# Moving the token scatters and two routing steps behind the first expert slot's set-up, and picking its token lists with bf16 matmuls

## The chip, the cores and the metric

One Trainium2 chip, one core. The metric is the device time of one launch in microseconds. The median of three runs of the kernel before is 1223.27 us.

## The reference, cut to what matters

Eight batches of eight heads, 576 tokens of 64 each, give 4608 tokens of 512 numbers. The kernel computes three things one after the other:

```python
q_s = softmax(q, axis=-1); k_s = softmax(k, axis=2)
x = einsum('bhsd,bhde->bhse', q_s, einsum('bhsd,bhse->bhde', k_s, v))   # x: 4608 x 512
logits = x @ w_gate + modality_bias[modality_id]                        # 8 experts
e_idx = argmax(logits, axis=1); gate_w = softmax(logits)[arange(N), e_idx]
out[mask] = gate_w[mask, None] * (relu(x[mask] @ w1[e]) @ w2[e])        # mask = (e_idx == e), 512 -> 1024 -> 512
return ((out @ m2_w1) * (out @ m2_w2)) @ m2_w3 @ m2_w_out
```

Each token goes to one expert only. So the kernel has to collect the tokens of an expert before it can multiply them.

## The kernel before

**The order of the work.** A small planner, `Plan`, takes every step with its engine, an estimated cost, the keys it reads and writes and a priority. It places the steps on the engines by these estimates, and each engine then runs its steps strictly in that order. A step that the planner puts too early therefore blocks what stands behind it on its engine.

**Attention and routing.** The tokens come in four chunks of two batches (`c` from 0 to 3). Each chunk has nine `attend` steps (L394 on): TensorE transposes the softmaxed queries (L399) and multiplies them (L412), ScalarE and VectorE evict the result (L422 to L425), SyncE stores x to DRAM (L429). After a chunk, `route(c)` (L441 on) adds up the logits and finds the argmax on VectorE (L450 to L458), gets every token's rank within its expert by ten bf16 matmuls (L463, L465) into PSUM bank 4, and computes positions (L468 to L472) and gate weights (L473 to L475). `scatters(c)` (L477) then writes the pairs (token number, gate weight) to `order_dram`, sorted by expert, with nine indirect DMAs of GpSimd (L436): 36 in all.

**Expert slots.** An expert slot (`slot`, L664 on) takes up to 512 tokens of one expert. SyncE loads the expert's weights (L697). GpSimd gathers the tokens' rows of x by four indirect DMAs (L706). ScalarE multiplies them by the gate weight (L710). TensorE transposes them (L726). To use the fast float32 form of matmul, weights and tokens are split in a high and a low part: by ScalarE (L677, L730) and by VectorE or, for two of eight W1 and W2 pieces, by GpSimd (L679, L731). Then come the first product with 96 matmuls (L743), the relu with its split (L747, L748), the second product with 96 matmuls (L763), and the stores (L773).

**The opening slots.** Slots 0 to 2 take only tokens of the first four batches, so they start before the attention of the later batches is finished. They don't read `order_dram`. `early_lists` (L564 on) builds their token lists on the chip. `A` (L595, six VectorE operations) has a one where a token's position modulo 128 fits a row, `same` (L599) where its block fits, `Bv` (L602, two operations) is `same` times the token number and times the gate weight. `pick` (L605 to L609) multiplies them, 18 float32 matmuls of 128x24 into bank 4:

```python
        for i, x in enumerate((ids, gate)):
            lv(vt_(n * nb), lambda i=i, x=x: V.tensor_tensor(Bv[:, :, :, i], same, x.unsqueeze(2).to_broadcast([128, n, nb]), op=ALU.mult), r=["same", "ids"] + [K("gate", c) for c in range(BEARLY // 2)], w=[K("Bv", i)])
```

The token numbers are then copied out (L612), which releases slot 0's gathers, and the gate weights too (L613). Slots from 3 on read their list from `order_dram` (L690), so the first of these loads needs all 36 scatters.

**The main program** (L836 to L905) adds, in this order: the four chunks with `route(c - 1)` inside chunk c, the scatters of chunks 0 to 2, slot 0, `route(3)`, the scatters of chunk 3, the table for the later slots (`main_table`, L615), slots 1 and 2, and the first steps of slots 3 and 4. Twelve conversions of dense weights (`doubles`, L779 on; GpSimd's part is L793) fill gaps. A branch follows (L886, L887), and after it the other slots and the dense products.

Of the kernel before, what the change touches and what calls it, by code (L numbers as in the profile page):

```python
# [20 lines left out]
E = 8  # L21
NT = 9
# [120 lines left out]
def body(tc, q, k, v, mod, wgate, mbias, w1, w2, m1, m2, w3, wo, out):  # L143
# [296 lines left out]

    def route(c):  # L441

# [6 lines left out]
        vv = lambda f, r=(), w=(), n=72: P.add("V", vt_(n), f, r=kk(r), w=kk(w))  # L449
        vv(lambda: V.tensor_tensor(l2_, l2_, rq_.unsqueeze(3).to_broadcast([128, H, NT, E]), op=ALU.mult), r=rqk, w=l2k, n=576)  # L450
        vv(lambda: V.tensor_reduce(l, l2_.rearrange("p h t e -> p t e h"), axis=AX.X, op=ALU.add), r=l2k, w=["l"], n=576)
# [38 lines left out]
    def vv(f, r=(), w=()):  # L490
        P.add("V", 0.15, f, r=list(r), w=["tbl"] + list(w), pri=tpri[0])
# [71 lines left out]
    def early_lists():  # L563
# [13 lines left out]

        A, Bv, same = part(n, 128), part(n, nb, 2), part(n, nb)
        io, ii, mf, mi, bf, bi, ids = part(128), part(128).bitcast(I32), part(n), part(n).bitcast(I32), part(n), part(n).bitcast(I32), part(n)
        first, fi, blocks = part(NE), part(NE).bitcast(I32), part(NE, 4)  # L580
# [18 lines left out]
        lv(vt_(n * nb), lambda: V.tensor_tensor(same, bf.unsqueeze(2).to_broadcast([128, n, nb]), blocks.rearrange("p a b -> p (a b)").unsqueeze(1).to_broadcast([128, n, nb]), op=ALU.is_equal), r=["blocks", "bf"], w=["same"])  # L599
        gate = tok[:, :, 1].bitcast(F32)  # L600
        for i, x in enumerate((ids, gate)):
            lv(vt_(n * nb), lambda i=i, x=x: V.tensor_tensor(Bv[:, :, :, i], same, x.unsqueeze(2).to_broadcast([128, n, nb]), op=ALU.mult), r=["same", "ids"] + [K("gate", c) for c in range(BEARLY // 2)], w=[K("Bv", i)])  # L602
        got = bank[4][:, 0 : 2 * nb]

# [3 lines left out]

        P.add("P", 2.5, pick, r=[K("A", c) for c in range(n // 3)] + [K("Bv", i) for i in range(2)] + kk, w=[K("bk", 4)])  # L609
        pv = got.rearrange("p (s t o) -> p s t o", s=NE, o=2)  # L610
        oks = [K("ord", i) for i in range(3)]
        lv(0.1, lambda: V.tensor_copy(ordt[:, 0:NE, :, 0], pv[:, :, :, 0]), r=[K("bk", 4)], w=oks)  # L612
        lv(0.1, lambda: V.tensor_copy(ordt[:, 0:NE, :, 1].bitcast(F32), pv[:, :, :, 1]), r=[K("bk", 4)], w=oks + kk)  # L613

# [49 lines left out]
    def slot(P, n, after=(), parts="lsab", T=None, again=False):  # L664
# [11 lines left out]
        def split(nm, i, raw, hi, lo, extra):  # L676
            P.add("S", sb_(512), lambda: SC.copy(hi(), raw()), r=[K(nm + "r", i), extra], w=[K(nm + "h", i)])  # L677
            e, g, c = (G, "G", gt_(512)) if i in (3, 7) else (V, "V", vt_(512))
            P.add(g, c, lambda: e.tensor_tensor(lo(), raw(), hi().bitcast(F32), op=ALU.subtract), r=[K(nm + "r", i), K(nm + "h", i), extra], w=[K(nm + "l", i)])  # L679

# [31 lines left out]
        if "s" in parts:  # L712
# [3 lines left out]
            for h in hs:  # L716
                for kp in range(2):
                    pb, ch = (5, 7)[kp], slice(TS * h, TS * h + TS)
                    p = bank[pb].rearrange("p (k t) -> p k t", k=2)
                    sl = slice(2 * kp, 2 * kp + 2)  # L720

                    def tr(kp=kp, p=p, h=h):
                        for kk in range(2):
                            for t in range(2):
                                c = 128 * (2 * kp + kk)
                                PE.transpose(p[:, kk, 128 * t : 128 * t + 128], xg[h][:, t, c : c + 128], ident)  # L726

                    P.add("P", 0.46, tr, r=[K("xg", h, 0), K("xg", h, 1)], w=[K("bk", pb)], pri=-230)
                    hi, lo = (lambda sl=sl, ch=ch: XT(0)[:, sl, ch]), (lambda sl=sl, ch=ch: XT(1)[:, sl, ch])
                    P.add("S", ps_(512), lambda hi=hi, p=p: SC.copy(hi(), p), r=[K("bk", pb), "Mb"], w=[K("xh", h, kp)], pri=-230)  # L730
                    P.add("V", vt_(512), lambda hi=hi, lo=lo, p=p: V.tensor_tensor(lo(), p, hi().bitcast(F32), op=ALU.subtract), r=[K("bk", pb), K("xh", h, kp)], w=[K("xl", h, kp, "t")], pri=-230)  # L731

# [106 lines left out]
    for c in range(4):  # L839
        load("k", c + 2)  # L840
        keys(c + 1)
        if c:
            route(c - 1)
# [16 lines left out]
    scats = lambda n: [K("scat", c) for c in range(NT * n // 2)]  # L860
    for c in range(3):
        scatters(c, ["Mb"])
    slot(P, 0)
    route(B // 2 - 1)
    scatters(3, ["Mb"])
    tpri[0] = 250
# [410 lines left out]
```

## Time and profile before

| what | value |
|---|---|
| median of three runs | 1223.27 us (1221.51 to 1226.41) |
| the profiled execution | 1225.3 us, span 1223.2 us |
| granted TensorE clock, mean of the span | 0.965 of full speed |
| TensorE busy | 1144.1 us, 94% |
| VectorE, ScalarE, GpSimd busy | 855.1 us (70%), 526.3 us (43%), 539.0 us (44%) |

The span is what the profile covers, and the time of the execution is 2.1 us longer. "Releaser" is what ended an engine's wait, as far as the profile can tell; "issue" means that the engine waited for nothing that the profile shows. A clock of 1.00 is TensorE's 2.4 GHz, 0.50 is 1.2 GHz.

### The profile page before, as it was taken

The numbers are of one execution on the slowest core, as the hardware profiler recorded it, in microseconds if no ns is written. First come the engines' busy times: TensorE is split into PE (matmuls) and PEld (weight loads), VectorE is DVE, ScalarE is ACT, GpSimd is POOL, SyncE is SP. The second block draws the span as 40 slices with busy tenths as digits, with TensorE's granted clock in tenths as the row PEclk, the third lists the DMA queues.
The fourth block names the chain that finished last, engine by engine and source line by source line (L and its number), as shares of the span: only waits on it lengthen the run. The fifth ranks groups of instructions, "written<-read, shape, count | busy, mean of one in ns | idle before, by whom it ended". The sixth has DMA issues, their size and how long they took to land.

```text
span 1223.2 us, 22923 instructions
## 1 busy us (share of the span) xinstructions
PE 1144.1 (94%) x8623; PEld 1040.8 (85%) x8623; DVE 855.1 (70%) x1435; ACT 526.3 (43%) x1003; POOL 539.0 (44%) x538
## 2 busy tenths in 40 slices
PE   3777879999989999999999999999999999999996
PEld 3666758778878888888987999999999999999996
DVE  6979768798468778778675757575666689765550
ACT  3545355434335444443463332424232445555550
POOL 0444248764133333323151355455555476443332
PEclk9878779999999999999999999999999999999998
DMA  9982464955246556445664334343443347987741
GB/s 355 390 309 81 136 204 145 187 178 211 99 137 206 168 181 197 157 164 181 208 204 141 100 110 136 101 141 110 128 124 116 97 147 246 341 266 236 234 140 51
DMA packets 156139, 216.00 MB, mean 177 GB/s; under 512 B 19790, under 2 KB 90994, under 8 KB 156018
## 3 DMA queue, kind: packets, MB, share of 16 engines
q1 hardware_dynamic: 148946, 195.00, 49.4%
q0 software_dynamic: 7072, 19.44, 5.2%
q8 instruction: 69, 1.13, 0.4%
q14 instruction: 52, 0.43, 0.1%
HBM read 156.35 MB, written 74.82 MB: 189 GB/s over the span
## 4 chain that ended last, share of the span: by engine, by line
PE 67%; DVE 2%; issue 1%; DMA 1%; ACT 0%; POOL 0%; SPq 0%; DVEq 0%; POOLq 0%; ACTq 0%
PE pb L1089 29%; PE pb L1222 14%; PE pb L763 12%; PE pb L743 10%; PE pb L982 2%; DVE ar L1016 2%; PE pb L726 1%; DMA ca<-p_dram 0%; DMA p_dram<-ca 0%; PE pb L969 0%; DVE ar L958 0%; POOL out_dram L1196 0%; DVE tt L958 0%; DVE al L958 0%; ACT al L957 0%
## 5 line engine op out<-in xcount | busy, mean ns | idle before, releaser
L1089 PE MATMUL pb<-al,ar 128*128 128x384 f32 x1728 | 309.3, 337 | 1.1 <-ACT sx L1095 0.8
L1089 PEld LDWEIGHTS pb<-al,ar 128*128 128x128 f32 x1728 | 301.7, 188 | 1.8 <-ACT sx L1095 1.1
L763 PE MATMUL pb<-ar 128*128 128x512 f32 (+1 forms) x960 | 215.2, 383 | 0.0
L743 PE MATMUL pb<-ar 128*128 128x512 f32 (+1 forms) x960 | 213.8, 383 | 1.0 <-DVE ar L748 0.5
L743 PEld LDWEIGHTS pb<-ar 128*128 128x128 f32 x960 | 174.4, 190 | 36.5 <-issue 1.3
L763 PEld LDWEIGHTS pb<-ar 128*128 128x128 f32 x960 | 174.3, 190 | 33.3
L1222 PE MATMUL pb<-ar 128*128 128x256 f32 x1512 | 182.6, 283 | 1.5 <-issue 0.7
L1222 PEld LDWEIGHTS pb<-ar 128*128 128x128 f32 x1512 | 181.8, 192 | 2.3 <-DVE ca L1236 0.8
L958 DVE TENSOR_TENSOR ar<-ca,ar 128x512 fp32r<-128x512 f32 x140 | 108.1, 779 | 53.6 <-ACT ar L957 42.9
L957 ACT CAST ar<-ca 128x512 fp32r<-128x512 f32 x140 | 86.2, 622 | 44.4 <-DMA ca<-p_dram 14.2
L747 ACT ACTIVATE ar<-pb 128x512 fp32r<-128x512 f32 (+1 forms) x80 | 46.1, 578 | 117.0 <-PE pb L743 110.6
L793 POOL TENSOR_TENSOR ca<-ca 128x512 f32<-128x512 f32 x40 | 56.2, 1405 | 85.3 <-DVE ca L792 71.3
L1095 ACT COPY sx<-pb 128x384 f32<-128x384 f32 x96 | 46.0, 481 | 91.8 <-PE pb L1089 55.5
L748 DVE SCALAR_TENSOR_TENSOR ar<-pb,ar 128x512 fp32r<-128x512 f32 (+1 forms) x80 | 52.6, 658 | 40.4 <-ACT ar L747 40.3
L330 POOL TENSOR_TENSOR kt<-kt,kr 128x384 f32<-128x384 f32 x36 | 44.3, 1267 | 76.0 <-ACT kr L324 76.0
L1123 POOL TENSOR_TENSOR ca<-ca 128x384 f32<-128x384 f32 x48 | 53.6, 1116 | 47.3 <-DVE ca L1123 47.3
L679 DVE TENSOR_TENSOR ar<-w2r,ar 128x512 fp32r<-128x512 f32 x60 | 46.1, 794 | 34.2 <-ACT ar L677 26.5
L1098 POOL TENSOR_TENSOR ca<-ca,sx 128x384 f32<-128x384 f32 x24 | 27.2, 1135 | 95.7 <-ACT sx L1095 95.7
L766 ACT COPY yo<-pb 128x512 f32<-128x512 f32 (+1 forms) x40 | 22.6, 565 | 107.7 <-PE pb L763 91.3
L679 POOL TENSOR_TENSOR ar<-w1r,ar 128x512 fp32r<-128x512 f32 x20 | 26.9, 1347 | 76.9 <-ACT ar L677 74.3
L1095 ACT COPY ca<-pb 128x384 f32<-128x384 f32 x48 | 23.0, 481 | 87.2 <-PE pb L1089 87.2
L706 POOL DMA_INDIRECT ca<-x_dram,ord x38 | 40.0, 1052 | 43.5 <-DVE ord L612 23.2
(276 smaller groups left out, 1816.4 us busy)
## 6 DMA issues: line engine op xcount, KB each, us to landing
p_dram<-ca SPq DMA_DIRECT2D x168, 192.0 KB
ca<-p_dram SPq DMA_DIRECT2D x126, 256.0 KB
w1r<-in_moe_w_dram SPq DMA_DIRECT2D x10, 2048.0 KB
w2r<-in_moe_w_dram SPq DMA_DIRECT2D x10, 2048.0 KB
ca<-in_moe_w_dram SPq DMA_DIRECT2D x32, 512.0 KB
kt<-in_k_dram SPq DMA_DIRECT2D x8, 1152.0 KB
qt<-in_q_dram SPq DMA_DIRECT2D x8, 1152.0 KB
vt<-in_v_dram SPq DMA_DIRECT2D x8, 1152.0 KB
```

The source lines that it names most:

```text
L679: P.add(g, c, lambda: e.tensor_tensor(lo(), raw(), hi().bitcast(F32), op=ALU.subtract), r=[K(nm + "r", i), K(nm + "h", i), extra], w=[K(nm ...
L743: PE.matmul(p(), lhsT=W1(i)[:, TURN[kk], ms], rhs=XT(z)[:, kk, cols], start=(kk == 0 and c == 0), stop=(kk == 3 and c == 2))
L747: P.add("S", ps_(N), lambda hh=hh, p=p: SC.activation(hh(), p(), AF.Relu), r=[K("bk", pb), "Mb"], w=[K("hh", h, m) for h in hs])
L748: P.add("V", vt_(N), lambda hh=hh, hl=hl, p=p: V.scalar_tensor_tensor(out=hl(), in0=p(), scalar=0.0, in1=hh().bitcast(F32), op0=ALU.max, o ...
L763: PE.matmul(p(), lhsT=W2(i)[:, f, ns], rhs=HT(y)[:, f, cols], start=(f == 0 and c == 0), stop=(f == 7 and c == 2))
L793: P.add("G", gt_(512), lambda: G.tensor_tensor(Tf, Tf, Qf, op=ALU.add), r=[K("Q", b)], w=[K("T", b)])
L957: P.add("S", (ps_ if psum else sb_)(n), lambda: SC.copy(hi(), src), r=sk, w=[hk])
L958: P.add("V", vt_(n), lambda: V.tensor_tensor(lo(), src, hi().bitcast(F32), op=ALU.subtract), r=list(sk) + [hk], w=[lk])
L1089: PE.matmul(bk(j), lhsT=Mt[:, f, a, i, m, t], rhs=X(y, x)[:, t], start=(fresh and t == 0 and n == 0), stop=(t == 1 and n == 2), skip_group ...
L1095: P.add("S", ps_(HB), lambda j=j, to=to: SC.copy(S(to), bk(j)), r=[bkk(j)], w=[sk(to)])
L1123: P.add(eng, c(HB), lambda: e.tensor_tensor(t[:, sl], x, y, op=op), r=kk, w=[k_])
L1222: PE.matmul(bk(j), lhsT=At[z][:, m, i, f], rhs=Bt[:, x, y, f], start=(fresh and f == 0 and n == 0), stop=(f == 3 and n == 2), skip_group_c ...
```

## The change

The numbers of lines move by 9 (L706 becomes L715, L743 becomes L752, and so on).

- The scatters of all four chunks are added after slot 0, and each reads the new key "cast". Slot 0's last GpSimd split of W1 writes that key.
- `route(2)` and `route(3)` are both added after slot 0. Their first step reads the new key "opened", which slot 0's split of the transposed tokens writes.
- `early_lists` breaks token numbers into two bf16 parts and gate weights into three. `A` and `Bv` are bf16. One VectorE operation of 1080 elements per partition makes `Bv`, and `pick` becomes 18 bf16 matmuls of 128x60. The parts are added up again by two reductions, one for the token numbers with a copy behind it, one for the gate weights.

```diff
-    def route(c):
+    def route(c, after=()):
...
-        vv(lambda: V.tensor_tensor(l2_, l2_, rq_.unsqueeze(3).to_broadcast([128, H, NT, E]), op=ALU.mult), r=rqk, w=l2k, n=576)
+        vv(lambda: V.tensor_tensor(l2_, l2_, rq_.unsqueeze(3).to_broadcast([128, H, NT, E]), op=ALU.mult), r=rqk + list(after), w=l2k, n=576)
...
-        A, Bv, same = part(n, 128), part(n, nb, 2), part(n, nb)
+        A, Bv, same = part(n, 64).bitcast(BF16), part(n, nb * 5 // 2).bitcast(BF16).rearrange("p a (b o) -> p a b o", o=5), part(n, nb)
...
+        lv(0.1, lambda: V.tensor_copy(xx[:, 0], ids), r=["ids"], w=["xx0"])
+        lv(0.1, lambda: V.tensor_tensor(xx[:, 1], ids, xx[:, 0], op=ALU.subtract), r=["ids", "xx0"], w=["xx1"])
+        lv(0.1, lambda: V.tensor_copy(xx[:, 2], gate), r=gk + kk, w=["xx2"])
+        lv(0.1, lambda: V.tensor_tensor(rest, gate, xx[:, 2], op=ALU.subtract), r=gk + ["xx2"], w=["rest"])
+        lv(0.1, lambda: V.tensor_copy(xx[:, 3], rest), r=["rest"], w=["xx3"])
+        lv(0.1, lambda: V.tensor_tensor(xx[:, 4], rest, xx[:, 3], op=ALU.subtract), r=["rest", "xx3"], w=["xx4"])
...
-        for i, x in enumerate((ids, gate)):
-            lv(vt_(n * nb), lambda i=i, x=x: V.tensor_tensor(Bv[:, :, :, i], same, ...
-        got = bank[4][:, 0 : 2 * nb]
+        lv(vt_(5 * n * nb), lambda: V.tensor_tensor(Bv, same.unsqueeze(3).to_broadcast([128, n, nb, 5]), xx.rearrange("p o a -> p a o").unsqueeze(2).to_broadcast([128, n, nb, 5]), op=ALU.mult), ...
+        got = bank[4][:, 0 : 5 * nb]
...
-        P.add("P", 2.5, pick, ...
+        P.add("P", 1.6, pick, ...
...
-        lv(0.1, lambda: V.tensor_copy(ordt[:, 0:NE, :, 0], pv[:, :, :, 0]), r=[K("bk", 4)], w=oks)
-        lv(0.1, lambda: V.tensor_copy(ordt[:, 0:NE, :, 1].bitcast(F32), pv[:, :, :, 1]), r=[K("bk", 4)], w=oks + kk)
+        lv(0.1, lambda: V.tensor_reduce(found, pv[:, :, :, 0:2], axis=AX.X, op=ALU.add), r=[K("bk", 4)], w=["found"] + kk)
+        lv(0.1, lambda: V.tensor_copy(ordt[:, 0:NE, :, 0], found), r=["found"], w=oks)
+        lv(0.1, lambda: V.tensor_reduce(ordt[:, 0:NE, :, 1].bitcast(F32), pv[:, :, :, 2:5], axis=AX.X, op=ALU.add), r=[K("bk", 4)], w=oks + kk)
...
-            P.add(g, c, lambda: e.tensor_tensor(...), r=[...], w=[K(nm + "l", i)])
+            P.add(g, c, lambda: e.tensor_tensor(...), r=[...], w=[K(nm + "l", i)] + (["cast"] if (n, nm, i) == (0, "w1", 7) else []))
...
-                    P.add("V", vt_(512), ..., w=[K("xl", h, kp, "t")], pri=-230)
+                    P.add("V", vt_(512), ..., w=[K("xl", h, kp, "t")] + ([K("opened")] if n == 0 else []), pri=-230)
...
-        if c:
+        if c in (1, 2):
             route(c - 1)
...
-    for c in range(3):
-        scatters(c, ["Mb"])
     slot(P, 0)
-    route(B // 2 - 1)
-    scatters(3, ["Mb"])
+    for c in (2, 3):
+        route(c, [K("opened")])
+    for c in range(4):
+        scatters(c, ["cast"])
```

The planner makes new orders out of this. On VectorE, in the run-up to `pick`, before:

```order
L451 TENSOR_REDUCE ca<-ca 128x72
L598 TENSOR_TENSOR qt_129<-qt_129 128x12
L452 TENSOR_TENSOR ca<-ca 128x72
L599 TENSOR_TENSOR qt_129<-qt_129 128x216
L453 TENSOR_REDUCE m_96<-ca 128x9
L602 TENSOR_TENSOR qt_129<-qt_129 128x216
L602 TENSOR_TENSOR qt_129<-qt_129,tid 128x216
```

and now, up to the copy that releases the gathers (L621):

```order
L605 TENSOR_SCALAR qt_129<-tab 128x3
L424 RECIPROCAL ca<-ca 128x8
L606 CAST qt_129<-qt_129 128x3
L425 TENSOR_TENSOR ca<-pp_83,ca 128x512
L607 TENSOR_TENSOR qt_129<-qt_129 128x12
L424 RECIPROCAL ca<-ca 128x8
L608 TENSOR_TENSOR qt_129<-qt_129 128x216
L425 TENSOR_TENSOR ca<-pp_82,ca 128x512
L609 TENSOR_TENSOR qt_129<-qt_129 128x1080
L385 TENSOR_TENSOR qs_134<-qt_130,qx_132 128x8x3x64
L620 TENSOR_REDUCE qt_129<-pb_75 128x12
L621 CAST ord<-qt_129 128x12
```

The steps of `route(2)` (L450 to L453 among them) are gone from here, and two evictions of attention (L424, L425) stand ahead of `pick`'s last operand instead; before, they stood behind it. A product of queries (L385) that stood behind the copy of the token numbers now stands ahead of it, and in the full order an L424 and a third L425 too, which this excerpt leaves out.

On TensorE around `pick`, as one piece of the difference (pp is an attention result, pb_75 is bank 4):

```order
 L399 MATMUL pb_78<-ident,qs_133 128x128 x4
-L607 MATMUL pb_75<-qt_129 128x24 x18
 L412 MATMUL pp_83<-bd_153,qT_137 64x73 x4
 L412 MATMUL pp_83<-bd_154,qT_137 64x73 x4
```

```order
 L412 MATMUL pp_82<-bd_153,qT_135 64x73 x4
 L412 MATMUL pp_82<-bd_154,qT_135 64x73 x4
+L614 LDWEIGHTS qt_129
+L614 MATMUL pb_75<-qt_129 128x60
```

The pair of L614 stands there 18 times. Two attends (64 matmuls, L412) that stood behind `pick` now stand ahead of it. The ten rank matmuls of `route(2)`, which came one transpose later, moved into slot 1's first product, beside those of `route(3)`.

On GpSimd, from slot 0's gathers on, before:

```order
L706 DMA ca<-x_dram,ord 128x512 x4
L436 DMA order_dram<-tid,pi 37376x2
L435 MEMSET nop 128x1
L436 DMA order_dram<-tid,pi 37376x2
L435 MEMSET nop 128x1
L436 DMA order_dram<-tid,pi 37376x2
L435 MEMSET nop 128x1
L436 DMA order_dram<-tid,pi 37376x2
L679 TENSOR_TENSOR ar<-w1r,ar 128x512 x2
```

and now:

```order
L715 DMA ca<-x_dram,ord 128x512 x4
L688 TENSOR_TENSOR ar<-w1r,ar 128x512 x2
L436 DMA order_dram<-tid,pi 37376x2
L435 MEMSET nop 128x1
L436 DMA order_dram<-tid,pi 37376x2
L715 DMA ca<-x_dram,ord 128x512 x2
```

The four scatters between slot 0's gathers and its splits of W1 moved behind the splits, where 36 now stand instead of 32. After the branch every engine's order is the same as before.

## Rows read from the trace of the kernel before

**Rows 1.** Stretches: length; PE, PEld, DVE, ACT, POOL busy; PE clock; DMA share; GB/s.
```profile
150.00:160.00 10.00, 4.36 (x71) 3.58 (x68) 1.75 (x8) 0.83 (x3) 6.85 (x10) 0.67 0.67 160
180.00:200.00 20.00, 19.98 (x96) 16.33 (x95) 19.97 (x33) 14.32 (x28) 15.21 (x18) 1.00 0.27 53
200.00:220.00 20.00, 20.00 (x93) 16.58 (x92) 11.01 (x17) 10.30 (x18) 16.68 (x22) 1.00 0.86 241
342.00:1223.00 881.00, 862.05 (x5121) 807.74 (x5121) 592.05 (x888) 368.26 (x694) 388.87 (x365) 0.99 0.52 165
```
**Rows 2.** Timeline of TensorE: start, length, engine, line, operation, count [idle before, releaser].
```profile
140.11 6.45 PE L607 MATMUL pb<-qt 128*128 128x24 f32 x36 [1.77 <-DVE qt L602]
...
149.63 0.52 PE L465 MATMUL pb<-oh,ones 128*128 128x72 bf16 x9
...
151.77 0.40 PE L412 MATMUL pp<-bd,qT 64*64 64x73 f32 x4 [0.20 <-issue]
...
159.79 0.28 PE L412 MATMUL pp<-bd,qT 64*64 64x73 f32 x1 [0.93 <-issue]
160.00 1.11 PE L399 MATMUL pb<-ident,qs 128*128 128x128 f32 x4
161.04 1.25 PE L412 MATMUL pp<-bd,qT 64*64 64x73 f32 x32
...
171.15 1.52 PE L743 MATMUL pb<-ar 128*128 128x512 f32 x2
```
**Rows 3.** Timeline of VectorE around `pick`.
```profile
134.85 1.95 DVE L595 TENSOR_TENSOR qt<-qt 128x384 f32<-128x384 f32 x4
...
137.57 1.20 DVE L451 TENSOR_REDUCE ca<-ca 128x72 f32<-128x576 f32 x1
...
139.68 0.38 DVE L602 TENSOR_TENSOR qt<-qt,tid 128x216 f32<-128x216 f32 x1
...
140.52 0.69 DVE L425 TENSOR_TENSOR ca<-pp,ca 128x512 f32<-128x512 f32 x1
...
146.60 0.17 DVE L612 CAST ord<-pb 128x12 int32<-128x12 f32 x1 [4.00 <-PE pb L607]
146.69 1.75 DVE L385 TENSOR_TENSOR qs<-qt,qx 128x1536 f32<-128x1536 f32 x1
```
**Rows 4.** Line L304, a VectorE operation of 1024 elements: durations in ns, minimum, median, maximum.
```profile
L304 DVE TENSOR_TENSOR tr<-kt x8: 1211/1222/1419, 6.5 to 95.3; 128x1024 f32<-128x1024 f32 x8
```
**Rows 5.** Timeline of GpSimd from slot 0's gathers on.
```profile
147.06 2.38 POOL L706 DMA_INDIRECT ca<-x_dram,ord  x1 [23.17 <-DVE ord L612]
...
152.25 0.95 POOL L706 DMA_INDIRECT ca<-x_dram,ord  x1 [0.30 <-issue]
153.50 1.00 POOL L436 DMA_INDIRECT order_dram<-tid,pi  x1 [0.30 <-issue]
...
154.81 0.98 POOL L436 DMA_INDIRECT order_dram<-tid,pi  x1 [0.19 <-issue]
```
**Rows 6.** DMA from 152 to 160: busy tenths in 0.2 us slices; packets, MB, share.
```profile
DMA  1547936659788999999999999975211000000000
...
q0 software_dynamic: 431, 0.98, 40.1%
...
q8 instruction: 1, 0.02, 0.8%
```
**Rows 7.** Timeline of ScalarE: slot 0's last scaling.
```profile
166.50 0.71 ACT L710 ACTIVATE ca<-ca,ord 128x512 f32<-128x512 f32 x1
```
**Rows 8.** Timelines of GpSimd, SyncE and ScalarE: the last scatter to slot 3's scaling.
```profile
254.85 0.97 POOL L436 DMA_INDIRECT order_dram<-tid,pi  x1
...
265.86 0.94 POOL L706 DMA_INDIRECT ca<-x_dram,ord  x1 [0.30 <-issue]
...
258.80 0.39 SPq L690 DMA_DIRECT2D ord<-order_dram  x1
...
277.36 0.71 ACT L710 ACTIVATE ca<-ca,ord 128x512 f32<-128x512 f32 x1
```

More of the change, by code (lines that the diff above doesn't have):

```diff
@@ L576, in part @@
             return t.rearrange(f"p ({' '.join(names)}) -> p {' '.join(names)}", **dict(zip(names[1:], shape[1:]))) if len(shape) > 1 else t
-        A, Bv, same = part(n, 128), part(n, nb, 2), part(n, nb)
-        io, ii, mf, mi, bf, bi, ids = part(128), part(128).bitcast(I32), part(n), part(n).bitcast(I32), part(n), part(n).bitcast(I32), part(n)
+        A, Bv, same = part(n, 64).bitcast(BF16), part(n, nb * 5 // 2).bitcast(BF16).rearrange("p a (b o) -> p a b o", o=5), part(n, nb)
+        io, ii, mf, mi, bf, bi, ids, rest = part(128), part(128).bitcast(I32), part(n), part(n).bitcast(I32), part(n), part(n).bitcast(I32), part(n), part(n)
+        xx = part(5, n // 2).bitcast(BF16)
         first, fi, blocks = part(NE), part(NE).bitcast(I32), part(NE, 4)
@@ L587, in early_lists @@
         lv(0.2, lambda: V.tensor_copy(io, ii), r=["io"], w=["iof"])
+        gate = tok[:, :, 1].bitcast(F32)
+        gk = [K("gate", c) for c in range(BEARLY // 2)]
         lv(0.1, lambda: V.tensor_copy(ids, tok[:, :, 0]), w=["ids"] + kk)
+        lv(0.1, lambda: V.tensor_copy(xx[:, 0], ids), r=["ids"], w=["xx0"])
[4 more added lines that the diff above has]
+        lv(0.1, lambda: V.tensor_tensor(xx[:, 4], rest, xx[:, 3], op=ALU.subtract), r=["rest", "xx3"], w=["xx4"])
         lv(0.1, lambda: V.tensor_scalar(mi, pos, 127, None, op0=ALU.bitwise_and), r=pk + kk, w=["mi"])
@@ L599, in early_lists @@
         lv(vt_(n * nb), lambda: V.tensor_tensor(same, bf.unsqueeze(2).to_broadcast([128, n, nb]), blocks.rearrange("p a b -> p (a b)").unsqueeze(1).to_broadcast([128, n, nb]), op=ALU.is_equal), r=["blocks", "bf"], w=["same"])
-        gate = tok[:, :, 1].bitcast(F32)
-        for i, x in enumerate((ids, gate)):
-            lv(vt_(n * nb), lambda i=i, x=x: V.tensor_tensor(Bv[:, :, :, i], same, x.unsqueeze(2).to_broadcast([128, n, nb]), op=ALU.mult), r=["same", "ids"] + [K("gate", c) for c in range(BEARLY // 2)], w=[K("Bv", i)])
-        got = bank[4][:, 0 : 2 * nb]
+        lv(vt_(5 * n * nb), lambda: V.tensor_tensor(Bv, same.unsqueeze(3).to_broadcast([128, n, nb, 5]), xx.rearrange("p o a -> p a o").unsqueeze(2).to_broadcast([128, n, nb, 5]), op=ALU.mult), r=["same"] + [f"xx{i}" for i in range(5)], w=["Bv"])
+        got = bank[4][:, 0 : 5 * nb]
         def pick():
@@ L607, in pick @@
                 PE.matmul(got, lhsT=A[:, j], rhs=Bv[:, j].rearrange("p a o -> p (a o)"), start=(j == 0), stop=(j == n - 1))
-        P.add("P", 2.5, pick, r=[K("A", c) for c in range(n // 3)] + [K("Bv", i) for i in range(2)] + kk, w=[K("bk", 4)])
-        pv = got.rearrange("p (s t o) -> p s t o", s=NE, o=2)
+        P.add("P", 1.6, pick, r=[K("A", c) for c in range(n // 3)] + ["Bv"] + kk, w=[K("bk", 4)])
+        pv = got.rearrange("p (s t o) -> p s t o", s=NE, o=5)
         oks = [K("ord", i) for i in range(3)]
-        lv(0.1, lambda: V.tensor_copy(ordt[:, 0:NE, :, 0], pv[:, :, :, 0]), r=[K("bk", 4)], w=oks)
-        lv(0.1, lambda: V.tensor_copy(ordt[:, 0:NE, :, 1].bitcast(F32), pv[:, :, :, 1]), r=[K("bk", 4)], w=oks + kk)
+        found = part(NE, 4)
+        lv(0.1, lambda: V.tensor_reduce(found, pv[:, :, :, 0:2], axis=AX.X, op=ALU.add), r=[K("bk", 4)], w=["found"] + kk)
+        lv(0.1, lambda: V.tensor_copy(ordt[:, 0:NE, :, 0], found), r=["found"], w=oks)
+        lv(0.1, lambda: V.tensor_reduce(ordt[:, 0:NE, :, 1].bitcast(F32), pv[:, :, :, 2:5], axis=AX.X, op=ALU.add), r=[K("bk", 4)], w=oks + kk)
     def main_table():
@@ L678, in split @@
             e, g, c = (G, "G", gt_(512)) if i in (3, 7) else (V, "V", vt_(512))
-            P.add(g, c, lambda: e.tensor_tensor(lo(), raw(), hi().bitcast(F32), op=ALU.subtract), r=[K(nm + "r", i), K(nm + "h", i), extra], w=[K(nm + "l", i)])
+            P.add(g, c, lambda: e.tensor_tensor(lo(), raw(), hi().bitcast(F32), op=ALU.subtract), r=[K(nm + "r", i), K(nm + "h", i), extra], w=[K(nm + "l", i)] + (["cast"] if (n, nm, i) == (0, "w1", 7) else []))
         if "l" in parts:
@@ L730, in slot @@
                     P.add("S", ps_(512), lambda hi=hi, p=p: SC.copy(hi(), p), r=[K("bk", pb), "Mb"], w=[K("xh", h, kp)], pri=-230)
-                    P.add("V", vt_(512), lambda hi=hi, lo=lo, p=p: V.tensor_tensor(lo(), p, hi().bitcast(F32), op=ALU.subtract), r=[K("bk", pb), K("xh", h, kp)], w=[K("xl", h, kp, "t")], pri=-230)
+                    P.add("V", vt_(512), lambda hi=hi, lo=lo, p=p: V.tensor_tensor(lo(), p, hi().bitcast(F32), op=ALU.subtract), r=[K("bk", pb), K("xh", h, kp)], w=[K("xl", h, kp, "t")] + ([K("opened")] if n == 0 else []), pri=-230)
         if "a" in parts:
```

## The prediction

> **What bounds the kernel now.** I read the busy time by stretches first, then the timelines of the engines at the places where TensorE is idle. From the branch to the end TensorE works 862 of 881 us [rows 1], and the diff moves nothing there. So a gain before the branch arrives at the end in full, and nothing can be gained after it. Between 180 and 220 TensorE is busy for 39.98 of 40 us [rows 1]: once slot 0 runs, TensorE is the bound. The loss lies ahead of that. Between 150 and 160 TensorE works 4.36 of 10 us [rows 1]. Slot 0's first product starts at 171.15 [rows 2], and whatever brings it forward is the gain.
>
> What does it wait for? The chain goes like this. `pick` takes TensorE 6.45 us from 140.11 on [rows 2]. VectorE copies the token numbers at 146.60, having waited 4.00 us for `pick` [rows 3]. The gathers start at 147.06, and the last is issued at 152.25 [rows 5]. The DMA engines work hard until about 157.8: in the slices of 0.2 us the digits drop from 9 at 157.6 on [rows 6]. Beside this chain TensorE has the last attends to do, and it does them very slowly: from 151.77 to 159.79 they come in small pieces, each after about a microsecond of "issue" [rows 2]. Nothing that the profile shows is awaited there. In the same stretch one packet of the instruction queue q8 moved, beside 431 packets of the gathers' and scatters' queue q0 with 40.1% of the DMA engines [rows 6]. I read this as an engine that had run out of instructions while the gathers held the DMA. The gathered tokens were there about 2 us before it ended.
>
> **The change, part by part.**
>
> *Pick's operands, on VectorE.* Six small operations are added ahead. One such costs at most 0.17 us [rows 3], so 1.0 in all; the six operations of `A` then end at 136.8 + 1.0 = 137.8 instead of 136.8. Output in bf16 might make `A` cheaper, and nothing in the trace shows that. I take 0.49 each as before. From there to the end of `Bv` 3.3 us passed (136.8 to 140.06) [rows 3]. Now stand there three small operations (0.5), two evictions (0.69 and a reciprocal each, some 1.7), `same` (0.38) and one product of 1080 elements. The nearest row is 1024 elements in 1.22 us [rows 4], so 1.28. That makes 3.9 at most. Starts lie closer than durations in this stretch, so I take 3.6: `pick` starts at 141.4 instead of 140.11, 1.3 us later. Bounds are 0.5 and 2.0.
>
> *Pick.* 36 float32 passes go, 18 bf16 matmuls come, of 60 columns. Nine bf16 matmuls of 8 to 72 columns (40 on average) took 0.52 us with their weight loads [rows 2]; 18 make 1.04, and I take 1.1. This ends at 142.5 instead of 146.56. If they cost half again as much, it is 143.0.
>
> *The copy.* Ahead of it now stands L385, 1.75 us [rows 3], which used to stand behind. It starts when VectorE is done with `Bv`, at 141.6, so most of it lies beside `pick`, and it ends at 143.4. A reduction, an eviction of 0.69 and the copy follow, about 1.0. The token numbers are out at 144.4, and as before 0.3 us later the gathers start: 144.7 instead of 147.06. **The gathers gain 2.4 us**, out of 5.3 us that `pick` itself saves, because VectorE takes the rest. Bounds: 1.5 and 3.5.
>
> *TensorE up to slot 0.* Two attends now run while VectorE makes `Bv`, in a gap that was 1.77 us of waiting [rows 2]. After `pick` five attends remain. At the slow level of the clock one takes 1.25 us and its four transposes 1.11 [rows 2], and three sets of transposes are left, so at most 5 x 1.25 + 3 x 1.11 = 9.6 us. That ends at 152.1 if instructions arrive in time. The gathered tokens come later than that, at 157.8 - 2.4 = 155.4. So the gathers and no longer the attends release the first product. From the start of the last scaling to the first product 4.65 us passed (166.50 to 171.15) [rows 2, 7]; with 0.1 in between, the first product starts at 160.15. **This gains 11.0 us.** The two terms overlap: the 2.4 us lie inside the 11.0.
>
> *The rank matmuls and routing of chunk 2.* Ten matmuls go from the busy place and come back in slot 1's first product: no net time. Its VectorE steps (L451 alone is 1.20) [rows 3], about 4 us, move into the stretch from 180 on, where VectorE is busy 19.97 of 20 us. In the next 20 us it is busy 11.01 [rows 1], so a backlog of 4 us is worked off there. TensorE may wait meanwhile for a split or for the one-hot of a rank matmul, which stands in its queue and blocks what is behind. I take **1.0 us lost**, with bounds of 0 and 4.
>
> *The scatters.* One costs 1.31 us of GpSimd with its memset (153.50 to 154.81) [rows 5]. Four go from between slot 0's gathers and splits. That part is worth nothing, as GpSimd then waits for the splits anyway. They come back behind, so 4 x 1.31 = 5.2 us more work stands ahead of slot 3's list. Cover is there: the last gather of slot 3 is issued at 265.86, slot 0's comparable one landed 5.5 us after its issue (152.25 to 157.8) [rows 5, 6], so at 271.4, and its scaling runs at 277.36 [rows 8], 6 us later. If that cover were gone, each further microsecond of scatters would delay slot 3 by one. SyncE's queue keeps its order but for slot 0's W2 load, which waits for the gathers and moves with them. I count 0.
>
> **Sum.** 1225.3 - 11.0 + 1.0 = 1215.3 for the profiled execution. That execution lies 2.0 us above the median, so the median becomes about **1213**.
>
> **Rule against row.** The row shows one instruction packet in the starved stretch and eight microseconds of TensorE in pieces [rows 2, 6]. The Trainium skill ("Runtime: NRT & Kernel Launch", Instruction fetch mechanics) says that instructions are fetched in blocks of 256 while the block before runs, and that crossing a block is mostly hidden. By that rule the stretch would cost nothing and the sum would stand at 1213. The Trainium skill ("DMA: Bandwidth & Descriptors", Queues, rings and completion order) also says that a DMA engine takes turns between queues packet by packet. By that rule a fetch that meets the gathers is slow again, which would make it the first rival's 1218. The measured stretch speaks for the second rule.
>
> **The rivals.**
>
> *The starved stretch comes back (1218).* It began 4.7 us after the first gather was issued (147.06 to 151.77) [rows 2, 5] and lasted 8.0. If it follows the gathers, it runs from 149.4 to 157.4. By 149.4 TensorE has done some 3.5 of its five attends. The other 1.4 cost 2.7 us more, up to 160.1, and 4.75 us later, at about 165, slot 0 starts. That is a gain of 6: 1225.3 - 6 + 1 - 2 = 1218. For it: the gathers are the same. Against it: `pick` has 36 instructions fewer and the ranks' 20 leave this place, so TensorE asks for the next instruction packet at another moment, which may miss the gathers. Only one packet did harm in the stretch shown.
>
> *Only the gathers' gain arrives (1222).* If something else holds the first product (the W1 splits on ScalarE, say), the gain is the 2.4 us less 1.0. Little speaks for that. That the change doesn't do what it says is excluded by the new orders, except that the bf16 pass might not be cheaper. Then `pick` keeps 6.45 us, and it would be slower by the 1.3 us of VectorE, within no change.
>
> *Slower (1233): the rank matmuls block TensorE.* Both routings wait for slot 0's tokens and then compete with the W1 and W2 splits on a VectorE that is full from 180 on [rows 1]. Their rank matmuls stand in slot 1's first product. If the one-hots are late there, TensorE stops, `main_table` is late, the 18 scatters behind them (24 us at 1.31) start late, and slot 3's list misses its 6 us of cover. Two routings at some 5 us each plus the backlog of 4 us and the 5.2 us of scatters make about 20 us, against 11 gained: 1223.3 - 11 + 1 + 20 = 1233. It decides from the point at which these waits together exceed 16 us. Against it: the 9 us that VectorE is free between 200 and 220.
>
> **How the numbers follow.** Forecast 0.54, starved stretch 0.23, only the gathers 0.12, slower 0.11. About 0.5%, 6 us, is what can be told from no change here: below 1217.2 is faster. The forecast with its bounds (the gathers 1.5 to 3.5, so 10 to 12 in place of 11; 0 to 4 in place of 1.0) runs from 1211 to 1217, nearly all faster; of the starved case four tenths are. So faster 0.61, no change 0.28, slower 0.11. The range reaches from 1208 to 1223, which takes in the forecast and both rivals that are faster or no change; it leaves out the slower case and a little on either side.
>
> **What would show it.** Right: 18 bf16 pairs in about 1.1 us, starting near 141.4; gathers at 144.7; TensorE's last attend by 152 to 153 with no row of "issue"; the first product near 160; the branch some 10 us earlier; nothing changed behind it. Wrong: "issue" pieces again in the attends (first rival), a first product still near 169, or TensorE waiting at L463 in slot 1 and ScalarE waiting for slot 3's list.

## The result, and the profile after

The changed kernel takes 1211.48 us (median of 6 runs, 1208.95 to 1216.31). The kernel before takes 1222.96 us in its six runs. The ratio is 0.9911 with a 95% interval of 0.9881 to 0.9940: faster by 11.5 us, clear of the 0.5%. The forecast was 1213 in a range of 1208 to 1223. The profiled execution of the changed kernel, at 1208.95 us, is the fastest of its six, so its trace shows a larger gain (16.3 us) than the medians do.

First the stretches of the changed kernel (columns as in [rows 1]):

```profile
150.00:160.00 10.00, 4.58 (x50) 3.44 (x48) 3.68 (x7) 5.41 (x14) 0.00 (x0) 0.63 0.87 199
160.00:180.00 20.00, 20.00 (x84) 16.26 (x83) 19.54 (x33) 12.16 (x24) 12.92 (x13) 0.93 0.77 220
...
328.00:1207.00 879.00, 860.46 (x5118) 806.16 (x5116) 591.48 (x888) 367.69 (x693) 388.73 (x365) 0.99 0.53 166
```

TensorE is as idle between 150 and 160 as before, but from 160 on it is busy without a gap. The stretch from the branch to the end is unchanged: it has 880.2 us in both traces (342.97 to 1223.2, and 326.98 to 1207.2). So the whole gain arises ahead of the branch, as forecast.

TensorE's timeline, the answer to [rows 2]:

```profile
138.40 1.51 PE L412 MATMUL pp<-bd,qT 64*64 64x73 f32 x64
141.00 0.67 PE L614 MATMUL pb<-qt 128*128 128x60 bf16 x18 [1.09 <-DVE qt L609]
...
149.28 1.56 PE L412 MATMUL pp<-bd,qT 64*64 64x73 f32 x64
151.16 0.33 PE L735 MATMUL pb<-ident,ca 128*128 128x128 f32 x1 [0.32 <-ACT ca L719]
...
158.26 2.21 PE L735 MATMUL pb<-ident,ca 128*128 128x128 f32 x8 [3.44 <-DVE ar L740]
160.12 15.06 PE L752 MATMUL pb<-ar 128*128 128x512 f32 x59
```

Two attends run ahead of `pick`. `pick` takes 0.67 us. The last attend ends at 150.84, and no row names "issue". After that TensorE waits for tokens, and slot 0's first product starts at 160.12. The gain up to there is 11.0 us.

VectorE and GpSimd, the answers to [rows 3] and [rows 5]:

```profile
133.76 2.90 DVE L604 TENSOR_TENSOR qt<-qt 128x384 bf16<-128x384 f32 x6
...
138.85 2.10 DVE L609 TENSOR_TENSOR qt<-qt 128x1080 bf16<-128x1080 f32 x1
...
143.30 0.16 DVE L621 CAST ord<-qt 128x12 int32<-128x12 f32 x1
```
```profile
143.75 1.13 POOL L715 DMA_INDIRECT ca<-x_dram,ord  x1 [20.00 <-DVE ord L622]
...
147.69 0.94 POOL L715 DMA_INDIRECT ca<-x_dram,ord  x1 [0.30 <-issue]
162.27 1.41 POOL L688 TENSOR_TENSOR ar<-w1r,ar 128x512 fp32r<-128x512 f32 x1 [13.64 <-ACT ar L686]
```

The gathers start 3.3 us earlier than in [rows 5], and no scatter follows them. What releases slot 0 shows on ScalarE: the third of the four scalings waits for gathered tokens, the fourth follows it, and TensorE's last eight transposes follow from these. The first product starts 2.74 us after the start of the last scaling.

```profile
156.29 0.72 ACT L719 ACTIVATE ca<-ca,ord 128x512 f32<-128x512 f32 x1 [3.28 <-DMA ca<-x_dram,ord]
157.38 0.72 ACT L719 ACTIVATE ca<-ca,ord 128x512 f32<-128x512 f32 x1
```

Behind slot 0's start the first product to the branch takes 166.86 us (160.12 to 326.98) instead of 171.82 (171.15 to 342.97). TensorE's waits there (without the wait of 4.5 us at the branch itself, which both kernels have) are 2.4, 0.5 and 0.3 us before, and 0.9, 0.3 and 0.2 us now.

### The profile page after: what moved, and what is told of

It reads as the page before. It is cut to its first block, busy times and chain, and to the rows that moved or that the text cites. A ratio compares the mean times of both kernels' runs of the same rounds, so it can differ in the third digit from the quotient of the medians.

```text
span 1207.2 us, 22895 instructions
## 1 busy us (share of the span) xinstructions
PE 1130.9 (94%) x8605; PEld 1029.5 (85%) x8605; DVE 859.3 (71%) x1441; ACT 526.3 (44%) x1003; POOL 538.7 (45%) x538
## 4 chain that ended last, share of the span: by engine, by line
PE 67%; DVE 3%; issue 1%; DMA 1%; ACT 0%; POOL 0%; SPq 0%; DVEq 0%; POOLq 0%; ACTq 0%
PE pb L1098 29%; PE pb L1231 13%; PE pb L772 12%; PE pb L752 10%; PE pb L991 2%; DVE ar L1025 2%; PE pb L735 1%; DMA ca<-p_dram 0%; DMA p_dram<-ca 0%; DVE ar L967 0%; PE pb L978 0%; POOL out_dram L1205 0%; DVE tt L967 0%; DVE al L967 0%; DVE ca L1121 0%
## 5 line engine op out<-in xcount | busy, mean ns | idle before, releaser
L752 PE MATMUL pb<-ar 128*128 128x512 f32 (+1 forms) x960 | 212.5, 381 | 0.2 <-DVE ar L757 0.2
L752 PEld LDWEIGHTS pb<-ar 128*128 128x128 f32 x960 | 173.9, 189 | 34.3 <-DVE ar L757 0.6
L688 POOL TENSOR_TENSOR ar<-w2r,ar 128x512 fp32r<-128x512 f32 x20 | 28.2, 1411 | 69.2 <-ACT ar L686 69.1
L1098 PE MATMUL pb<-thm,ar 128*128 128x384 f32 x288 | 59.0, 340 | 0.0
```

What stands on the lines that cost most here:

```text
L752: PE.matmul(p(), lhsT=W1(i)[:, TURN[kk], ms], rhs=XT(z)[:, kk, cols], start=(kk == 0 and c == 0), stop=(kk == 3 and c == 2))
L1098: PE.matmul(bk(j), lhsT=Mt[:, f, a, i, m, t], rhs=X(y, x)[:, t], start=(fresh and t == 0 and n == 0), stop=(t == 1 and n == 2), skip_group ...
```

## The experiments

The question was which part of the change brought the 11 us, and what made the starved stretch of [rows 2]. In all of them "first product" is the first matmul of L743, which is L752 where the line numbers are those of the changed kernel.

**The token lists alone.** The kernel before with the `early_lists` of the changed one.

```diff
-        A, Bv, same = part(n, 128), part(n, nb, 2), part(n, nb)
+        A, Bv, same = part(n, 64).bitcast(BF16), part(n, nb * 5 // 2).bitcast(BF16).rearrange("p a (b o) -> p a b o", o=5), part(n, nb)
...
-        P.add("P", 2.5, pick, ...
+        P.add("P", 1.6, pick, ...
```

> The kernel before with the bf16 token lists alone; routes and scatters stay where they were, so four scatters again follow slot 0's gathers. Theory P (the place in TensorE's instruction stream at which the gathers' traffic meets it makes the starved stretch): pick is 36 instructions shorter and the gathers start some 3 us earlier, near 144, so the stretch is missed; first product near 161 to 163, time 1212 to 1216. Theory S (the four scatters behind the gathers make the starved stretch): issue pieces among the attends again, of some 8 us; first product near 167, time 1219 to 1222.

Measured: 1223.08 us, ratio 0.9992 (0.9976 to 1.0009). This is no change, though `pick` takes 1.06 us. TensorE behind it:

```profile
143.07 1.06 PE L614 MATMUL pb<-qt 128*128 128x60 bf16 x18 [3.58 <-DVE qt L609]
...
151.35 1.22 PE L412 MATMUL pp<-bd,qT 64*64 64x73 f32 x21
153.50 0.35 PE L412 MATMUL pp<-bd,qT 64*64 64x73 f32 x4 [0.93 <-issue]
...
157.79 0.49 PE L412 MATMUL pp<-bd,qT 64*64 64x73 f32 x2 [0.44 <-issue]
...
169.89 8.50 PE L752 MATMUL pb<-ar 128*128 128x512 f32 x29
```

VectorE makes the operand late, and TensorE waits 3.58 us for it. The gathers start at 145.24, 1.8 us earlier than before. The pieces with "issue" are back, and the first product starts 1.3 us earlier only. Theory P's number falls. Theory S has the pieces right, but its time (1219 to 1222) is missed too.

**The moves alone**, float32 lists.

```diff
-        if c:
+        if c in (1, 2):
             route(c - 1)
...
-    for c in range(3):
-        scatters(c, ["Mb"])
     slot(P, 0)
-    route(B // 2 - 1)
-    scatters(3, ["Mb"])
+    for c in (2, 3):
+        route(c, [K("opened")])
+    for c in range(4):
+        scatters(c, ["cast"])
```

> The kernel before with the moved routes and scatters alone; the token lists stay in float32. Pick still takes about 6.4 us, gathers start at 145.5 to 147. Theory S: with the scatters gone the attends run without issue pieces and the gathers release slot 0: first product near 162 to 163, 1214 to 1216. Theory P: it depends on the place alone; the rank matmuls' 20 instructions have left this stretch, so the stretch may come back: first product 167 to 171, 1219 to 1223.

Measured: 1212.99 us, ratio 0.9906 (0.9881 to 0.9931). **The moves bring the whole gain.** The time lies just below theory S's, and theory P falls. The first product starts at 161.00. Float32 `pick` starts at once behind two attends and is cheaper than in [rows 2]:

```profile
139.41 4.77 PE L607 MATMUL pb<-qt 128*128 128x24 f32 x36
...
147.43 0.52 PE L412 MATMUL pp<-bd,qT 64*64 64x73 f32 x5 [0.20 <-issue]
...
161.00 17.17 PE L743 MATMUL pb<-ar 128*128 128x512 f32 x68
```

A few short issue rows are left (0.2 to 0.4 us each).

**The changed kernel and the moves again, on one chip.** No edit.

> The changed kernel again, as the partner of the next run on the same chip. Theory P+ (the bf16 pick is worth its earlier gathers, 0.9 to 3 us, once the scatters are out of the way): 1 to 3 us below the moves with the float32 pick. Theory P0 (the pick is worth nothing here): within 1 us of it.

> The moves with the float32 pick again. Theory P+: 1 to 3 us above the changed kernel. Theory P0: within 1 us of it. Both: 0.988 to 0.993 of the kernel before.

Measured: 1212.92 us, ratio 0.9922 (0.9899 to 0.9946), against 1213.04 us, ratio 0.9930 (0.9911 to 0.9948). Theory P0 fits: with the moves made, no gain of the bf16 lists can be told from zero. The six runs of each kernel spread over 9 and 5 us, so the 1 to 3 us of theory P+ are not excluded. The traces show where most of the shorter `pick` goes. `pick` is 4 us shorter (0.68 instead of 4.76) but starts at 142.01 instead of 140.01. The gathers gain 0.5 us (144.76 and 145.27), and the first products are at 161.26 and 159.87.

**The scatters alone.** Routes and lists as before.

```diff
-    for c in range(3):
-        scatters(c, ["Mb"])
     slot(P, 0)
     route(B // 2 - 1)
-    scatters(3, ["Mb"])
+    for c in range(4):
+        scatters(c, ["cast"])
```

> The kernel before with the scatters alone behind slot 0's W1 splits; routes and token lists as before. TensorE's stream up to slot 0 is as before. Theory P: the starved stretch of some 8 us stays, first product near 171, time 1221 to 1225. Theory S: it is gone, first product near 163, 1214 to 1216. Both: no more than 2 us lost behind slot 0.

Measured: 1219.09 us, ratio 0.9965 (0.9953 to 0.9977), between the two theories. The first product starts at 165.43. The issue pieces are there, but closer together (0.73 us instead of 1.45) and only from 151.97 to 154.6:

```profile
151.97 0.36 PE L412 MATMUL pp<-bd,qT 64*64 64x73 f32 x4 [0.17 <-issue]
152.70 0.35 PE L412 MATMUL pp<-bd,qT 64*64 64x73 f32 x5 [0.38 <-issue]
153.44 0.36 PE L412 MATMUL pp<-bd,qT 64*64 64x73 f32 x5 [0.39 <-issue]
154.18 0.41 PE L412 MATMUL pp<-bd,qT 64*64 64x73 f32 x10 [0.37 <-issue]
```

**TensorE's program shifted by 128 instructions.**

```diff
         def over_partitions():
+            for _ in range(64 if c == 0 else 0):
+                PE.matmul(bk[:, 0:16], lhsT=ones16, rhs=ones16[:, 0:16], start=True, stop=True)
```

> The kernel before with 64 small bf16 matmuls and their weight loads (128 instructions) at the very start of TensorE's program, before its first 9.5 us of waiting for data are over, so they cost nothing by themselves. Everything behind them stands 128 instructions later. Theory P: the starved stretch moves or vanishes, time 1213 to 1218 if it vanishes. Theory S: the stretch stays at 151 to 160, and the time is 1221 to 1225.

Measured: 1223.93 us, ratio 1.0000 (0.9983 to 1.0017). The stretch is there again. The first gather is at 151.32, and the first issue row follows 4.67 us later, as in [rows 2, 5] (4.71 us):

```profile
155.99 0.35 PE L414 MATMUL pp<-bd,qT 64*64 64x73 f32 x4 [0.16 <-issue]
...
161.04 0.28 PE L414 MATMUL pp<-bd,qT 64*64 64x73 f32 x1 [0.93 <-issue]
```

So a shift by 128 instructions does not move the stretch away from the gathers: theory P falls.

**The routes alone.** The moves without "cast", so that scatters may follow the gathers (the diff is against the moves).

```diff
+    for c in range(2):
+        scatters(c, ["Mb"])
     slot(P, 0)
     for c in (2, 3):
         route(c, [K("opened")])
-    for c in range(4):
-        scatters(c, ["cast"])
+    for c in (2, 3):
+        scatters(c, ["Mb"])
```

> The kernel before with routes 2 and 3 behind slot 0's tokens; scatters are free to run behind the gathers again (five stand there instead of four), token lists in float32. Theory S (scatters behind the gathers keep TensorE short of instructions): issue pieces 1.45 us apart until 1 to 2 us after the fifth scatter, some 8 us in all; first product 165 to 168. Theory R (the moved route alone frees TensorE and VectorE, scatters do no harm): first product near 161 to 162 and 1212 to 1215. By S the time is 1217 to 1221.

Measured: 1216.54 us, ratio 0.9964 (0.9946 to 0.9983). The time lies between the two theories' ranges, above R's and just below S's. Five scatters stand behind the gathers, from 149.79 on, and still there is no issue row and the first product is early, as by theory R:

```profile
148.07 1.67 PE L412 MATMUL pp<-bd,qT 64*64 64x73 f32 x32
150.92 0.74 PE L412 MATMUL pp<-bd,qT 64*64 64x73 f32 x32 [1.18 <-DVE ca L425]
...
159.25 15.35 PE L743 MATMUL pb<-ar 128*128 128x512 f32 x60
```

Up to slot 0 this trace has the whole gain (the execution, at 1214.48 us, is 2 us faster than its kernel's median). It gives part back behind: there TensorE waits 6.7 us, and in the moves' repeated trace 2.8. The waits of this kernel from 159 to the branch (line, releaser, us, times, longest):

```profile
PE pb L743 <- DVE ar L748: 2.2, 1, 2.2
PE pb L726 <- DVE ar L731: 1.8, 1, 1.8
PE pb L726 <- ACT ca L710: 1.7, 2, 1.4
PE pb L463 <- DVE cnt L469: 1.0, 1, 1.0
```

**The changed kernel with the scatters put back.** The same edit on the changed kernel.

> The changed kernel with the wait for the W1 splits taken off the scatters, so that five run right behind slot 0's gathers. Theory S: the issue pieces are back, 1.45 us apart, from about 148.4 (4.7 us after the first gather) to about 158; first product 164 to 167 instead of 160; time 1215 to 1219. Theory R: as the changed kernel, 1210 to 1213.

Measured: 1215.12 us, ratio 0.9953 (0.9939 to 0.9967); the changed kernel on that chip has 0.9922. No issue row, first product at 160.24, and again waits of 2.2, 1.7, 1.4 and 1.0 us behind it. So theory S falls as to the starved stretch, though the time lies in its range and not in R's. The two intervals overlap, so this pair alone does not settle what the scatters' wait is worth. The pair of the routes alone (0.9964) and the moves (0.9930) on the same chip points the same way, by some 4 us. In these traces the waits lie between 175 and 219 us, in slots 0 and 1.

**Nine scatters behind slot 0's gathers**, instead of four, in the kernel before.

```diff
-lambda t=t: scatter(pi_[c][:, t : t + 1], tid[:, c, t])
+lambda t=t: [scatter(pi_[c][:, u : u + 1], tid[:, c, u]) for u in (range(3, NT) if (c, t) == (0, 3) else () if c == 0 and t > 3 else (t,))]
```

> The kernel before with nine scatters instead of four right behind slot 0's gathers (the planner's step of the fourth one issues the chunk's last five as well). Theory S (TensorE gets instructions in small pieces for as long as GpSimd issues indirect DMAs, and a stretch that starts 4.7 us after the first gather ends 1 to 2 us after the last scatter): the issue pieces last until 165 to 167, first product at 175 to 178, time 1226 to 1230. Theory G (the gathers' data alone set the end of the stretch; scatters do no harm): the pieces end near 160 as before, first product 171 to 173 and 1222 to 1225.

Measured: 1222.43 us, ratio 1.0017 (0.9999 to 1.0034). Both theories forecast pieces, and the trace shows none: the attends run at full speed beside gathers and scatters.

```profile
150.74 0.74 PE L412 MATMUL pp<-bd,qT 64*64 64x73 f32 x32 [0.61 <-DVE ca L425]
...
152.00 0.74 PE L412 MATMUL pp<-bd,qT 64*64 64x73 f32 x32
...
156.96 0.90 PE L726 MATMUL pb<-ident,ca 128*128 128x128 f32 x3 [2.87 <-ACT ca L710]
...
164.94 13.03 PE L743 MATMUL pb<-ar 128*128 128x512 f32 x48
```

The last attend stands behind a transpose that waits 2.87 us for a scaled tile. This first product is 6 us earlier than in [rows 2], while the median is not lower. So scatters do not by themselves make the pieces. (One execution is traced for each kernel.)

**Gathers held until the attends are over**, with the scatters behind the W1 splits. From the kernel with the scatters alone, which had pieces, this differs only by the hold.

```diff
+    P.add("G", 0.2, lambda: G.tensor_copy(nop, rq[1][:, 0, NT - 1 : NT]), r=[K("rq", 1, NT - 1)], w=["held0"])
     slot(P, 0)
```

> The kernel before with its scatters behind the W1 splits, and with a small GpSimd copy ahead of slot 0's gathers that reads the last attend's result, so that GpSimd issues no indirect DMA until the attends are over; route 2, token lists and TensorE's order as before. Theory D (TensorE's attends come in pieces with issue gaps only where they run beside the gathers' traffic): no issue row in the attends behind pick; the last attend ends 8 to 14 us after pick's end, and since the gathers then need 8 to 10 us and the rest 4.75, first product at 166 to 174 and time 1218 to 1227. Theory I (the pieces come from TensorE's own instruction stream, whatever the DMA does): issue pieces again some 5 us behind pick, last attend 15 us or more after pick's end, first product past 174.

Measured: 1227.61 us, ratio 1.0043 (1.0024 to 1.0063), just above theory D's range. There is no issue row; the last attend ends at 156.10, 9.0 us after the end of `pick`:

```profile
155.36 0.74 PE L412 MATMUL pp<-bd,qT 64*64 64x73 f32 x32 [0.36 <-ACT ca L422]
165.17 0.47 PE L726 MATMUL pb<-ident,ca 128*128 128x128 f32 x1 [9.07 <-ACT ca L710]
...
173.73 11.54 PE L743 MATMUL pb<-ar 128*128 128x512 f32 x41
```

TensorE then waits 9.07 us for the tokens. Waiting costs more than the stretch did. From the first gather (157.75) to the first product it takes 16.0 us.

**The token lists ahead of the evictions**, on the changed kernel, with the changed kernel as its partner.

```diff
-        lv = lambda cost, f, r=(), w=(): P.add("V", cost, f, r=list(r), w=list(w))
+        lv = lambda cost, f, r=(), w=(): P.add("V", cost, f, r=list(r), w=list(w), pri=-300)
```

The same priority is given to `pick`.

> The changed kernel with a higher priority for the token lists' steps, so that VectorE makes the operand of pick ahead of the two evictions and TensorE runs pick ahead of the two attends. Theory E (what the gathers gain arrives at slot 0, as the prediction has it): gathers start 1.5 to 3 us earlier, near 142, first product 157.5 to 159, time 1 to 3 us below the changed kernel. Theory F (attends must be done before TensorE runs short of instructions, 4.7 us after the first gather): more attends now lie behind the gathers, issue pieces come back, first product 160 to 164, time equal to the changed kernel or up to 4 us above it.

> The changed kernel as the partner of the run before on the same chip: 0.988 to 0.995 of the kernel before, first product 160 to 161.5, no issue pieces among the attends.

Measured: 1212.04 us, ratio 0.9917 (0.9889 to 0.9945), against 1209.92 us, ratio 0.9913 (0.9885 to 0.9940): the same. `pick` runs at 137.46, two to five us earlier than in the other traces of the changed kernel. But the gathers start at 142.09, and in the partner at 142.40, so nearly nothing of this reaches them. VectorE's own order takes it: two evictions and a reduction of queries (L384) stand ahead of the reduction that the copy needs (L620).

```profile
138.55 1.29 DVE L425 TENSOR_TENSOR ca<-pp,ca 128x512 f32<-128x512 f32 x2
139.76 1.74 DVE L384 TENSOR_REDUCE qx<-qt 128x24 f32<-128x1536 f32 x1
141.42 0.17 DVE L620 TENSOR_REDUCE qt<-pb 128x12 f32<-128x24 f32 x1
```

The first product is at 159.65, and in the partner at 157.11. Two attends now stand behind slot 0's first transposes:

```profile
151.29 0.90 PE L735 MATMUL pb<-ident,ca 128*128 128x128 f32 x3 [0.61 <-ACT ca L719]
152.13 2.23 PE L412 MATMUL pp<-bd,qT 64*64 64x73 f32 x64
...
159.65 20.82 PE L752 MATMUL pb<-ar 128*128 128x512 f32 x85
```

Theory E is not tested by this, since the gathers gained only 0.3 us. Theory F's time is right, but its pieces did not come. The partner itself has its first product 3 us earlier than expected, and it shows a single issue row among its attends, 1.01 us, against its expectation.

## Why the prediction was right, and where it was wrong

**The sum was right up to slot 0.** First product at 160.12, forecast 160.15; `pick` from 141.00 (141.4) in 0.67 us (1.1); gathers at 143.75 (144.7); last attend over at 150.84 (152.1 at most); the branch 16.0 us earlier (some 10), the rest unchanged. That the first product agrees to 0.03 us is luck. The last scaling starts at 157.38 where the sum has 155.5, and from there to the first product it takes 2.74 us where the sum took 4.65 from [rows 2, 7]: two errors of 1.9 us that cancel. Two other traces of the changed kernel have the first product at 161.26 and 157.11. What held is the chain: the attends are over before the tokens come, and the tokens release slot 0.

**The step that names the cause was wrong.** The prediction made the gathers' 2.4 us the work of `pick`, out of 5.3 us that `pick` saves, and tied the rest to the starved stretch that vanishes. The runs show no gain of the new `pick` that can be told from zero: alone it gives 0.9992, and on top of the moves the two times are the same. Two terms were mis-sized. The product of 1080 elements takes 2.10 us, where 1.28 was taken from [rows 4]. And float32 `pick` costs 6.45 us in [rows 2] at a mean granted clock of 0.62, behind a wait. In the moves alone, right behind two attends, it costs 4.77 us at 0.86, and in the routes alone 4.20 us at 1.00.

**The gain comes from both moves, in about equal parts.** By the medians the routes alone give 0.9964 and the scatters alone 0.9965, some 4.4 us each (their intervals are about 2 us wide to either side), and the two together 0.9906 and 0.9930. The prediction gave neither a gain of its own; that the rank matmuls leave this place it named only as a reason why the starved stretch might be missed.

**Up to slot 0 the moved `route(2)` stands out.** The prediction counted it as no net time on TensorE and some microseconds of loss on VectorE. But its VectorE steps and its ten rank matmuls stood among the last attends. From the first gather to the first product it takes 14.6 to 17.6 us in the eight profiled executions with moved routes, and 18.1 to 24.7 in the five that have `route(2)` in its old place and gathers that are not held. The routes alone have their first product at 159.25. Part of the 11.9 us to [rows 2] is the choice of executions: this one is 2 us faster than its median, that of the kernel before 2 us slower.

How the move does it is argued, not shown. In the routes alone VectorE evicts the attend ahead of `pick` at 137.39, and before at 140.52 [rows 3]. Two attends then fit ahead of `pick`, and five instead of seven are left behind it:

```profile
137.39 0.69 DVE L425 TENSOR_TENSOR ca<-pp,ca 128x512 f32<-128x512 f32 x1 [0.17 <-DVE qt L597]
```

This order alone does not decide: with the token lists ahead of the evictions seven attends stand behind `pick`, and the first product comes as early (159.65). Nor is VectorE short of time behind `pick` in the kernel before. It stands idle for 7.95 us while the attends come in pieces:

```profile
159.39 0.20 DVE L424 RECIPROCAL ca<-ca 128x8 f32<-128x8 f32 x1 [7.95 <-issue]
```

No run parts the VectorE steps of `route(2)` from its rank matmuls.

**The scatters were priced at nothing, and are worth some 2 to 5 us.** Alone the change of their place gives 0.9965; there the trace has the gain ahead of slot 0, where the pieces are fewer. Taken back from the changed kernel it costs about 0.3%, which is not clear of the noise by itself, and there the trace has waits behind slot 0. Their cover at slot 3 held, as forecast: the last scatter is issued at 243.35, 11.5 us earlier than in [rows 8], and slot 3's gathers at 254.67 no longer wait for their list.

**Behind slot 0 a loss of 1 us was forecast.** The three executions of the changed kernel take 166.9, 169.9 and 168.8 us from first product to branch, against 171.8 before, so this is a gain of 2 to 5 us. The rank matmuls do wait for VectorE as the prediction feared, by 0.3, 2.8 and 0.4 us.

**The reading of the starved stretch falls.** The prediction took it for an engine out of instructions, with a packet of the queue q8 held up by the gathers. In the trace of the lists alone the pieces end at 158.28. Up to 158.3 the DMA view has no packet of q8. The two queues that moved from 152.5 to 158.3 were

```profile
q1 hardware_dynamic: 1046, 0.52, 63.8%
q0 software_dynamic: 305, 0.56, 36.2%
```

and in the trace of the scatters alone no packet of q8 moved during the pieces either. So it is not the arrival of an instruction packet that ends the stretch. Whether TensorE lacked instructions in another way no trace shows. What the Trainium skill says of fetching ("Runtime: NRT & Kernel Launch", Instruction fetch mechanics: the crossing of a block is mostly hidden) is therefore not contradicted by [rows 2]. But an earlier place of the same trace speaks against it:

```profile
66.84 0.70 PE L349 MATMUL pb<-vp,kt 64*64 64x65 f32 x11 [3.83 <-issue]
```

Here the DMA view has one packet of q8 that starts between 64.4 and 65.7, and none from 62.9 to 64.4 or from 65.7 to 66.8. The program shifted by 128 instructions breaks the same line (L351 there) at other matmuls, with waits of 3.05 us ahead of 33.96 and 2.16 us ahead of 66.02, while its pieces beside the gathers stay. So a wait for a packet looks here like one long gap whose place depends on the program, and the starved stretch has not this form. That the packet ends these gaps is a reading of the times, not tested by a run. The turns that a DMA engine takes between queues, packet by packet (the Trainium skill, "DMA: Bandwidth & Descriptors", Queues, rings and completion order), from which the prediction derived a slow fetch, explain nothing that these traces show of the stretch.

**What stays open** is what makes the pieces. Runs of them came only beside slot 0's gathers (none with the gathers held, in one execution). A single issue row stands elsewhere too, such as 1.03 us ahead of an attend at 164.38 in the lists alone. And gathers are not enough (no pieces with nine scatters, none in the routes alone), and neither the shift of the program nor the scatters decide.

## What to carry to other kernels

When several engines feed one start, price a moved step by what it leaves behind as well: taking a step out of a busy run-up helped more than making the step on the critical chain seven times shorter. A duration read at the slow clock level belongs to that place only; look at what runs ahead of it before crediting its removal. And run each part of a change alone: a sum that comes out right to 0.1 us can still name the wrong part. One trace of each kernel is one execution, and here two executions of one kernel differ by 4 us at slot 0; what a part is worth is read from the medians.

## What the runs showed of the hardware that was not expected

- The VectorE product of 1080 elements with bf16 output and two broadcast operands took 2.10 us (1.94 ns per element), against 1.22 us for 1024 elements in float32 [rows 4]. The six `A` operations cost the same with bf16 output as with float32 (2.90 us for six, 1.95 for four [rows 3]).
- The same 36 float32 passes took 4.20 to 7.88 us. With 4.20, in the routes alone, the granted clock was 1.00. With 7.88, in the trace with the gathers held, they lay in a stretch at clock 0.50 (first their rows, then their stretches):

```profile
139.90 4.20 PE L607 MATMUL pb<-qt 128*128 128x24 f32 x36
139.20 7.88 PE L607 MATMUL pb<-qt 128*128 128x24 f32 x36 [1.37 <-DVE qt L602]
```
```profile
139.90:144.10 4.20, 4.20 (x43) 4.20 (x39) 2.21 (x2) 0.59 (x3) 0.00 (x0) 1.00 1.01 345
140.00:146.00 6.00, 6.00 (x30) 6.00 (x30) 1.69 (x8) 0.00 (x0) 0.00 (x0) 0.50 0.64 258
```

- Attends beside four gathers were cut into pieces of 1 to 10 matmuls at distances of about 0.73 or 1.45 us, and in other executions ran at 0.74 us per attend beside the same gathers.
